# Linear attention and gated convolution on one core: transposes of Q and K in 64-row form into two PSUM banks, steps moved between engines, zero fills as steps, a new order

## The chip, the core and the metric

The kernel runs on one NeuronCore of a Trainium2 chip. The metric is the device time of one execution in microseconds (us), as the median of several runs. The engines are TensorE (PE, with its weight loads as PEld), VectorE (DVE), ScalarE (ACT), GpSimd (POOL) and SyncE (SP). Each works through its own instructions in order and waits for the others by semaphores. Loads that change fp32 to bf16 are issued from POOL's queue; stores are issued from SP's.

## The reference

B = 8 batches, H = 8 heads, S = 576 tokens, D = 64, F = 128 features. The first half is an attention with feature maps, the second a gated unit with a causal convolution of five taps:

```python
def phi(x):
    proj = np.einsum('bhsd,df->bhsf', x, w_phi)
    proj = proj - np.max(np.abs(proj), axis=-1, keepdims=True)
    return np.concatenate([np.exp(proj), np.exp(-proj)], axis=-1)
q_p, k_p = (phi(q), phi(k))
kv = np.einsum('bhsf,bhsd->bhfd', k_p, v)
z = np.sum(k_p, axis=2)
num = np.einsum('bhsf,bhfd->bhsd', q_p, kv)
den = np.einsum('bhsf,bhf->bhs', q_p, z)[..., None] + 1e-06
...
for k in range(K):
    gate_pre += conv_w[k][None, None, :] * xp[:, k:k + S, :]
gate = 1.0 / (1.0 + np.exp(-gate_pre))
val = x @ w_val
return (gate * val @ w_out).astype(np.float32)
```

x is the attention's output, num / den, with the heads side by side (8 x 64 = 512 columns).

## The kernel before

**Units.** Two heads of one batch make a unit (`hp` 0 to 3 in a batch, so 32 units, numbered batch x 4 + `hp`). Of a head's 576 tokens, each of 64 partitions holds 9 neighbouring ones; the two heads of a unit fill the 128 partitions. Eight of the nine token planes go through the unit steps; the ninth planes of a batch's four units go together through steps with an `e` in their names. A number behind a step's name is its unit; for the `e` steps, loads and the second half it is the batch.

**The steps of a unit.** `T` (line 335) transposes its K and Q on PE: eight products of 128 columns against the identity `ident`, into one PSUM bank as bf16. `Tc` copies the 1024 columns to SBUF. `PK` and `PQA` (line 348) multiply by `W2` (w_phi twice, one copy for each half of the rows) with tokens on the partitions. From these DVE takes the largest absolute value of each token: `mKa`, `mKb` for the two banks of K, `mQ` for Q (all line 365). ACT makes `Ka`, `Kb` (line 429), the exponentials of K, each step two instructions, and `E` (line 414), the scales by the maxima. `V` on POOL (lines 454 and 458) multiplies V with the scales. `KV` (line 476) is the product of K's features and V; its last operand, for the ninth planes, is a tile `VZ` of which half must be zero (memsets in line 214). `KVM` copies the result to SBUF. For Q, `PQa` and `PQb` (line 518) make the features with features on the partitions; a nop on SP (`WQ`) stands between them because different row halves write one bank. `DMQ` (line 400) spreads the maxima of Q on a doubled identity `id64`, `SH` (line 534) subtracts them by a product that accumulates, and `Qp`, `Qm` (line 548) are the exponentials. `NUM` (line 566) multiplies Q's features with the copy of `KV`; `RCP` and `XN` on DVE divide; `XP` (line 596) transposes and `XC` copies into `XT`, the input of the second half.

**The second half**, one per batch: `HL` copies the last tokens of the planes in `XT` to where the convolution reads them (SBUF to SBUF). `GA` (line 767) is the convolution as 80 small products, `THx` and `THy` (line 791) the gate on ACT, `VA` (line 802) the product with w_val, `GV` (line 823) gate times value on DVE, `OUT` (line 831) the product with w_out, `OE` (lines 851 on ACT, 853 on DVE) its way out of PSUM, `ST` the store on SP. `WC` brings w_val into another order, SBUF to SBUF.

**What sets the order.** `ORDER` is one text of some 1240 words. Each is a step with its number, behind `@` its PSUM bank or banks, and behind `:` its engine where there is a choice (`P` POOL, `D` DVE, `A` ACT). The program issues the steps in the order of this text, so each engine gets its instructions in that order. `FL` (line 244) is a product that nothing reads, put where PE would be idle. Loads are steps too: `LK`, `LQ`, `LV`, `LE` for a whole batch, `LKa`, `LKb` and so on for parts of the first batch; unit 0's K and Q come first, by other queues (line 195).

Of the kernel before, what the change touches and what calls it, by code (L numbers as in the profile page):

```python
# [29 lines left out]
mQ0 CW0 mKa0 FL13@4 LVa0 Ka0 DMQ0:D Tce1:D mKb0 T1@7 PKe1@4 Kb0 Tc1:D FL15@0 PQA1@6 mQe1 FL6@2 E0 mKe1 KTe1  # L30
mQ1 DG0:P LKb0 PK1@1,2 T4@0 mKb1 PQa0@6 WQ0 PQb0 SH0 Tc4:D FL4@3 T5@0 FL1@3 LE1 DMQ1:D Ka1 PQA4@4 mKa1 Kb1 LE0
V0:P PK4@2,3 Qm0 E1 Qp0 Tc5:D FL19@1 FL12@0 PQA5@6 mKa4 DMQe1:P Ee1 FL18@1 mQ4 PQa1@0 LQb0 PQea1@4 WQ1 PQb1
SH1 Ka4 LV1 FL7@2 Kb4 FL17@2 WQe1 PQeb1 FL11@2 SHe1 DMQ4:D mQ5 Qm1 Qp1 FL8@2 Te0@2 DMQ5:D T2@6 mKb4 Tce0:D Qe1
PKe0@0 PQea0@2 WQe0 Tc2:A mKe0 T3@7 Ee0 mQe0 Ve1:P DMQe0:D E4 V1:P KTe0 PQeb0 FL10@4 FL9@4 PQA2@5 Tc3:D LWV0
SHe0 mQ2 PK2@4,7 FL5@0 Qe0 Ve0:P LVb0 PK3@0,1 KV1@5 mKb2 V4:P PQa4@2 mKb3 WQ4 KV0@6 PQb4 Ka2 Kb2 KVM1:D SH4
mKa2 Kb3 KVM0:D mKa3 PQA3@4 DMQ2:P NUM1@6 mQ3 LWO0 Qm4 RCP1 T6@1 XN1 LK2 KV4@4 PQa2@6 WQ2 E2 PQb2 Qp4 SH2
PQa3@2 E3 DMQ3:D XP1@5 Tc6:D Ka3 WC3:D V2:P NUM0@0 KVM4:D WQ3 PQb3 SH3 XC1:D KV2@4 Qm2 Qp2 V3:P Qp3 PK5@5,6
Qm3 RCP0 WC2:D XN0 KVM2:D XP0@7 KV3@4 mKb5 mKa5 XC0:D NUM2@0 KVM3:A NUM3@2 RCP2 XN2 Ka5 NUMe0@7 PQa5@0 WQ5
# [5 lines left out]
Qm7 Tc9:D mQ8 LK3 RCP6 PKe2@6 E8 XN6 OUT0_2@5 mKe2 NUM7@2 mQe2 LQ3 Tc11:D RCP7 OE0_2:A XN7 OUT0_1@4 KTe2
PQA9@0 PK9@6,7 PQa8@2 WQ8 LQ4 OUT0_0@5 Ee2 OE0_1:A DMQ8:P mQ9 XP7@4 Kb9 mKa9 V8:P XP6@1 OE0_0:A mKb9 T10@0
NUMe1@5 XC6:D Ve2:P XC7:D PQb8 SH8 DMQe2:P RCPe1 XNe1 Ka9 OUT0_3@7 E9 Tc10:D KV8@1 Qp8 PK10@0,6 PQea2@4 WQe2
OE0_3:D Qm8 V9:P KVM8:A XPe1@7 mKa10 PQeb2 SHe2 NUM8@2 XCe1:A DMQ9:P Qe2 KV9@7 PQA10@4 HL1:P mKb10 RCP8 XN8
KVM9:D PQa9@1 LV3 XP8@3 Ka10 mQ10 XC8:D Kb10 WQ9 PQb9 SH9 T12@0 Te3@5 Qp9 GA1@6,3 Tc12:D Tce3:D PK11@0,5 Qm9
# [25 lines left out]
XN20 OUT3_0@5 LV6 Qm21 OUTe1@7 Kb22 mKa22 OEe1:D GA4@0,3 DMQ22:D OE3_0:A Ka22 THx4 PK23@7,6 STe1 Te6@5 mKa23
V21:P THy4 VA4_0@2 E22 mKb23 T24@0 Tce6:D GV4_0 KV21@1 E23 ST2_1 PQa22@4 PQA23@2 Kb23 Tc24:D WQ22 LK7 PQb22
SH22 PK24@6,0 KVM21:D VA4_2@1 Ka23 mQ23 NUM21@2 mKa24 GV4_2 Qm22 RCP21 Kb24 XN21 VA4_3@7 VA4_1@1 LQ7 mKb24
Qp22 V22:P KV22@2 Ka24 XP20@5 XP21@0 V23:P GV4_3 GV4_1 PQa23@6 PQA24@3 KVM22:A LE7 DMQ23:P E24 XC21:A LV7
# [30 lines left out]
def kernel(  # L108
# [102 lines left out]
    for i in range(3):  # L211
        VZs.append(const.tile([P, 2, 2, HP, E1], BF16, name=f"VZ{i}"))
        for h2 in range(2):
            nc.vector.memset(VZs[i][row(h2), :, 1 - h2, :, :], 0.0)
# [761 lines left out]
```

## Time and profile before

| | |
|---|---|
| median of 3 runs | 233.06 us (232.55 to 233.15) |
| profiled execution, own time | 233.09 us |
| its span, first to last instruction | 231.3 us |
| mean granted clock of TensorE | 0.975 |
| instructions of PE / PEld / DVE / ACT / POOL | 3853 / 3888 / 347 / 385 / 192 |
| bytes moved | 26.12 MB |

The span is 1.8 us shorter than the execution's own time. Busy time of PE counts each product until its modelled end, and neighbouring products overlap, so a busy PE isn't yet one at its peak rate. On the other engines, too, an instruction starts a little before the one ahead of it has ended, so a group's busy time is less than its count times its mean. The second part of the page is in 40 slices of 5.8 us each; its row of the granted clock shows full speed but for slices 2 and 3, about 11.6 to 23 us, at half.

### The profile page before, as it was taken

How to read it: one execution, taken by the hardware profiler on the slowest of the kernel's cores; microseconds unless marked ns; L12 is line 12 of the kernel's file. 1: busy time of each engine (PE TensorE's matmuls, PEld its weight loads, DVE VectorE, ACT ScalarE, POOL GpSimd, SP SyncE). 2: the span in 40 equal slices, each digit the busy share in tenths (PEclk: the TensorE clock that was granted, in tenths of full speed). 3: DMA queues.
4: the chain of work that ended last, by engine and by line, in shares of the span. 5: the costliest groups of instructions: out<-in, count | busy, mean ns of one | idle time of the engine just before them, and what ended most of it. 6: DMA issues, size and time to landing. Idle time of an engine off the chain costs nothing.

```text
span 231.3 us, 9094 instructions
## 1 busy us (share of the span) xinstructions
PE 204.6 (88%) x3853; PEld 134.4 (58%) x3888; DVE 198.2 (86%) x347; ACT 192.2 (83%) x385; POOL 158.9 (69%) x192
## 2 busy tenths in 40 slices
...
GB/s 139 213 178 11 138 117 113 114 100 116 38 180 128 167 31 100 127 131 152 172 146 110 105 35 81 18 149 254 206 34 74 94 3 4 27 191 107 95 179 141
DMA packets 27843, 26.12 MB, mean 113 GB/s; under 512 B 5653, under 2 KB 22933, under 8 KB 27802
## 3 DMA queue, kind: packets, MB, share of 16 engines
...
q14 instruction: 11, 0.09, 0.1%
...
## 4 chain that ended last, share of the span: by engine, by line
PE 62%; DVE 17%; ACT 6%; DMA 5%; issue 5%; POOL 1%; DVEq 0%; POOLq 0%; SPq 0%
PE PS L831 11%; PE PS L802 10%; PE PS L348 6%; PE PS L566 6%; DMA kN<-in_k_dram 5%; PE PS L335 5%; PE PS L476 5%; DVE MQ L365 5%; ACT KT L429 3%; PE PS L767 3%; PE PS L518 3%; DVE MK L365 3%; PE PS L596 3%; PE PS L534 2%; DVE XN L586 2%
## 5 line engine op out<-in xcount | busy, mean ns | idle before, releaser
L429 ACT ACTIVATE KT<-PS 128x512 bf16<-128x512 f32 x128 | 68.9, 630 | 10.2 <-DVE MK L365 9.0
L454 POOL TENSOR_TENSOR VT<-vN,E 128x1024 bf16<-128x1024 bf16 x28 | 53.3, 1903 | 26.2 <-ACT E L414 24.1
L548 ACT ACTIVATE QT<-PS 128x1024 bf16<-128x1024 f32 x64 | 64.0, 1064 | 3.1 <-PE PS L683 1.2
L365 DVE TENSOR_REDUCE MK<-PS 128x4 f32<-128x512 f32 x64 | 42.4, 681 | 2.2 <-PE PS L348 1.7
L365 DVE TENSOR_REDUCE MQ<-PS 128x8 bf16<-128x1024 f32 x32 | 39.0, 1218 | 3.8 <-PE PS L348 3.1
L802 PE MATMUL PS<-XT,WVAL 128*128 128x512 bf16 x113 | 30.4, 380 | 1.4 <-issue 0.5
L831 PE MATMUL PS<-WOUT,GV 128*128 128x512 bf16 x113 | 30.3, 380 | 1.0 <-issue 0.3
L400 POOL TENSOR_TENSOR DM<-id,MQ 128x512 bf16<-128x512 bf16 x24 | 25.0, 1042 | 4.6 <-DVE MQ L365 4.3
L348 PE MATMUL PS<-W,T 64*128 64x128 bf16 x512 | 25.0, 220 | 2.8 <-DVE MKe L365 1.0
L476 PE MATMUL PS<-VT,KT 128*128 128x65 bf16 x512 | 24.8, 194 | 2.0 <-DVE KVS L150 1.0
L476 PEld LDWEIGHTS <-KT 128*128 128x128 bf16 x512 | 21.8, 98 | 5.2 <-DVE KVS L150 1.4
L348 PEld LDWEIGHTS <-T 64*128 64x128 bf16 x512 | 16.8, 95 | 12.8 <-issue 8.3
L823 DVE SCALAR_TENSOR_TENSOR GV<-GATE,PS 128x512 bf16<-128x512 bf16 x32 | 21.0, 680 | 3.5 <-ACT GATE L791 3.1
L586 DVE TENSOR_TENSOR XN<-PS,RCP 128x512 bf16<-128x512 f32 x32 | 22.1, 690 | 1.0
L566 PE MATMUL PS<-KVS,QT 128*128 128x65 bf16 x512 | 21.0, 193 | 0.9 <-DVE T L150 0.5
L566 PEld LDWEIGHTS <-QT 128*128 128x128 bf16 x512 | 18.5, 97 | 5.3 <-issue 1.9
L480 PE MATMUL PS<-VZ,KTe 128*128 128x65 bf16 x128 | 21.4, 192 | 0.0
L150 DVE COPY T<-PS 128x1024 bf16<-128x1024 bf16 x30 | 20.4, 682 | 0.4 <-PE PS L335 0.4
L454 POOL TENSOR_TENSOR VZ<-vE,Ee 64x512 bf16<-64x512 bf16 x16 | 16.7, 1042 | 3.1 <-ACT Ee L414 2.4
L518 PE MATMUL PS<-T,W 64*128 64x256 bf16 x128 | 18.0, 278 | 0.6 <-DVE XN L586 0.2
L802 PEld LDWEIGHTS <-WVAL 128*128 128x128 bf16 x128 | 10.9, 97 | 11.7 <-issue 1.2
L791 ACT ACTIVATE GATE<-PS 128x1024 bf16<-128x1024 f32 x16 | 15.7, 1033 | 2.4 <-PE PS L767 2.4
...
## 6 DMA issues: line engine op xcount, KB each, us to landing
...
```

The costliest lines, as they stand in the source:

```text
L348: (nc.tensor.matmul(PS[:, banks[g], jj * F:(jj + 1) * F], T[row(g), n, jj, :, :].rearrange("p a t -> p (a t)"), W2[row(g), :], start=True, ...
L365: nc.vector.tensor_reduce(dst, x, AX.X, ALU.max, apply_absolute_value=True)
L400: engines[eng].tensor_tensor(u.DM[:, :, :], id64[:, :].unsqueeze(1).to_broadcast([P, n, 64]), u.MQ[:, :, :].rearrange("p j g -> p (j g)"). ...
L429: nc.scalar.activation(u.KT[:, ft, par, :, :].rearrange("p b f -> p (b f)"), PS[:, u.PK[par], :], AF.Exp, scale=1.0 if ft == 0 else -1.0,)
L454: engines[eng].tensor_tensor(dst[:, :, :, 0:D], x.unsqueeze(1).to_broadcast([rows, 2, n, D]), e.unsqueeze(3).to_broadcast([rows, 2, n, D]) ...
L476: nc.tensor.matmul(o, u.KT[:, ft, y % 2, h2 * 2 + y // 2, :], u.VT[:, ft, h2 * 4 + y, :], start=(y == 0), stop=False,)
L518: return nc.tensor.matmul(PS[:, u.PQ + a, :].rearrange("p (j g t) -> p g j t", g=2, t=64)[:, g, :, :], W2[row(g), :], u.T[row(g), 1, :, a, :],
L548: nc.scalar.activation(u.QT[:, ft, :, :, :].rearrange("p a n t -> p a (n t)"), half(u.PQ, 512), AF.Exp, scale=1.0 if ft == 0 else -1.0,)
L566: (nc.tensor.matmul(u.NUM[:, jj // 2, x * E1:(x + 1) * E1], u.QT[:, ft, jj // 2, 4 * h2 + 2 * (jj % 2):4 * h2 + 2 * (jj % 2) + 2, :].rearr ...
L586: nc.vector.tensor_tensor(u.XN[:, :, :, :], numview(u)[:, :, :, 0:D], u.RCP[:, :, :].unsqueeze(3).to_broadcast([P, 2, 4, D]), ALU.mult,)
L802: nc.tensor.matmul(PS[:, m.val[r], :], WVAL[:, dt, r, :], xt(b)[:, dt, 4:12, :].rearrange("p n t -> p (n t)"), start=(dt == 0), stop=(dt = ...
L831: nc.tensor.matmul(PS[:, m.out[j], :], m.GV[:, r, j * P:(j + 1) * P], WOUT[:, r, :], start=(r == 0), stop=(r == 3),)
```

## The change

**Transposes.** `T` uses the two halves of the partitions apart: 16 products of 64 columns in place of eight of 128, the products of rows 0 to 63 into one bank and those of rows 64 to 127 into the next. Of each bank 256 words (512 bf16 columns) are used. `Tc` copies the same 1024 columns from two banks.

**Steps moved between engines.** All 32 `DMQ` and the 8 `DMQe` are on POOL (8 and 1 were on DVE), and so is the last `HL` (was on DVE). The four `WC` are on ACT (two were on DVE, two on POOL). `ND`, which makes `id64`, goes from POOL to DVE. Steps that read PSUM move as follows, from DVE to ACT or back: `Tc` on ACT 4 (was 2), `Tce` 3 (0), `KVM` 19 (17), `XC` 4 (8), `OE` 18 (22), `OEe` 3 (2); the rest of each is on DVE.

**Zero fills.** The six memsets of the `VZ` tiles on DVE at the start become three steps `ZV` of two instructions each: two steps on ACT as copies of a zero tile, one on DVE.

**Unread products.** `FL` is called 16 times (was 20), at other places; the eight ahead of the list stay.

**The list** is new as a whole. Its first line before and after, and the diff of the functions:

```diff
-CK0 CQ0 LQ1 T0@5 Tc0:A W0 LKa0 LK1 FL3@2 IF0:D FL2@1 ND0:P PQA0@6 PK0@0,2 FL16@1 FL0@1 FL14@1 LQa0 TP0@1 Te1@3
+LKa0 LK1 FL9@7 LQa0 LQ1 IF0:D LKb0 CK0 LVa0 TP0@4 CW0 DG0:P CQ0 T0@0 ZV0:A Tc0:A ND0:D W0 PQA0@1 mQ0 DMQ0:P
...
         VZs.append(const.tile([P, 2, 2, HP, E1], BF16, name=f"VZ{i}"))
-        for h2 in range(2):
-            nc.vector.memset(VZs[i][row(h2), :, 1 - h2, :, :], 0.0)
...
+    def op_ZV(i, eng):
+        for h2 in range(2):
+            z = VZs[i][row(h2), :, 1 - h2, :, :]
+            if eng == "A":
+                nc.scalar.activation(
+                    z.rearrange("p f h e -> p f (h e)"),
+                    zero[row(h2), 0:HP * E1].unsqueeze(1).to_broadcast([64, 2, HP * E1]), AF.Copy,
+                )
+            else:
+                engines[eng].memset(z, 0.0)
...
     def op_T(i, bank):
         u = units[i]
-        u.Tps = PS[:, bank[0], :].bitcast(BF16)
+        u.Tps = half(bank[0], 256).bitcast(BF16)
+        tv = u.Tps.rearrange("p h (n x a t) -> p h n x a t", n=2, x=2, a=2)
         for n, name in enumerate(("k", "q")):
             for jj in range(4):
-                nc.tensor.transpose(
-                    u.Tps.rearrange("p (n h x a t) -> p n x a h t", n=2, h=2, x=2, a=2)[:, n, jj % 2, jj // 2, :, :],
-                    tok(name, u.b)[:, u.hp, jj * P:(jj + 1) * P], ident[:, :],
-                )
+                for h2 in range(2):
+                    nc.tensor.transpose(
+                        tv[:, h2, n, jj % 2, jj // 2, :],
+                        tok(name, u.b)[row(h2), u.hp, jj * P:(jj + 1) * P], ident[row(h2), row(h2)],
+                    )
...
     def op_Tc(i, eng):
...
-        copy(eng, u.T[:, :, :, :, :].rearrange("p n y a t -> p (n y a t)"), u.Tps)
+        copy(
+            eng, u.T[:, :, :, :, :].rearrange("p n (h x) a t -> p h n (x a t)", h=2),
+            u.Tps.rearrange("p h (n e) -> p h n e", n=2),
+        )
```

POOL at the start of the program, before. `kN` and `qN` are the bf16 tiles of K and Q; 128x576 is one unit's, 128x4x576 a batch's (here batch 1), 128x2x576 the last two units' of batch 0.

```order
L279 DMA qN<-in_q_dram 128x4x576
L279 DMA kN<-in_k_dram 128x576
L279 DMA kN<-in_k_dram 128x4x576
L241 TENSOR_TENSOR id_132<-ident 128x64
L279 DMA qN<-in_q_dram 128x576
L261 TENSOR_TENSOR id_134<-ident 128x32
L262 TENSOR_TENSOR id_134<-id_134,ident 128x32
L263 TENSOR_TENSOR id_134<-id_134,ident 128x32
L264 TENSOR_TENSOR DIAG<-id_134,cwT 128x640
L279 DMA kN<-in_k_dram 128x2x576
L282 DMA vE<-in_v_dram 128x4x64 x2
L454 TENSOR_TENSOR VT<-OS,E 128x16x64
```

The same place after.

```order
L288 DMA kN<-in_k_dram 128x4x576
L288 DMA qN<-in_q_dram 128x576
L288 DMA qN<-in_q_dram 128x4x576
L288 DMA kN<-in_k_dram 128x2x576
L270 TENSOR_TENSOR id_128<-ident 128x32
L271 TENSOR_TENSOR id_128<-id_128,ident 128x32
L272 TENSOR_TENSOR id_128<-id_128,ident 128x32
L273 TENSOR_TENSOR DIAG<-id_128,cwT 128x640
L414 TENSOR_TENSOR DM<-id_126,MQ 128x512 x2
L288 DMA qN<-in_q_dram 128x2x576
L291 DMA vE<-in_v_dram 128x4x64 x2
L414 TENSOR_TENSOR DM<-id_126,MQ 128x512
```

Unit 1's K, issued even ahead of these rows, and its Q now go out before batch 1's Q, which was the first load and is now behind them. The last two units' K of batch 0 go out ahead of `DIAG`, which waits for DVE. Three `DMQ` stand ahead of the first `V`, where there was none.

ACT from its first activation on, before (`qN` and `T` of unit 0, then exponentials `KT`, scales `E`; `KTe` is that of batch 1's ninth planes).

```order
L235 ACTIVATE qN<-QT 128x576
L148 ACTIVATE T<-PS 128x1024
L429 ACTIVATE KT<-PS 128x512 x4
L414 ACTIVATE E<-MK 128x8 x2
L669 ACTIVATE KTe<-PS 128x512 x2
L429 ACTIVATE KT<-PS 128x512 x4
L548 ACTIVATE QT<-PS 128x1024
```

And after.

```order
L244 ACTIVATE qN<-QT 128x576
L233 ACTIVATE VZ_121<-zero 64x2x260 x2
L148 ACTIVATE T<-PS 128x2x2x256
L233 ACTIVATE VZ_123<-zero 64x2x260 x2
L443 ACTIVATE KT<-PS 128x512 x8
L428 ACTIVATE E<-MK 128x8 x4
L443 ACTIVATE KT<-PS 128x512 x4
```

Four zero fills come in, the exponentials of units 0 and 1 stand in one piece, and those of batch 1's ninth planes no longer stand between them.

POOL at the end of the program, before: the last `V` and `DMQ` steps and `HL6` (`XT`).

```order
L454 TENSOR_TENSOR VT<-vN,E 128x16x64
L458 CAST VT<-E 128x16
L150 COPY XT_119<-XT_119 128x4x4x63
L400 TENSOR_TENSOR DM<-id_132,MQ 128x512 x2
L454 TENSOR_TENSOR VT<-vN,E 128x16x64
L458 CAST VT<-E 128x16
L454 TENSOR_TENSOR VT<-vN,E 128x16x64
L458 CAST VT<-E 128x16
```

And after.

```order
L472 CAST VT<-E 128x16
L414 TENSOR_TENSOR DM<-id_126,MQ 128x512
L468 TENSOR_TENSOR VT<-vN,E 128x16x64
L472 CAST VT<-E 128x16
L414 TENSOR_TENSOR DM<-id_126,MQ 128x512
L150 COPY XT_119<-XT_119 128x4x4x63
```

The last `DMQ` now follows the last `V`, and `HL7` is POOL's last instruction; before, it was DVE's.

More of the change, by code (lines that the diff above doesn't have):

```diff
@@ L28 @@
 ORDER = """
-CK0 CQ0 LQ1 T0@5 Tc0:A W0 LKa0 LK1 FL3@2 IF0:D FL2@1 ND0:P PQA0@6 PK0@0,2 FL16@1 FL0@1 FL14@1 LQa0 TP0@1 Te1@3
[L30 to L38, printed above, removed]
@@ L44 @@
[L44 to L48, printed above, removed]
@@ L74 @@
[L74 to L77, printed above, removed]
-PKe6@1 mQ24 XC20:A KTe6 WQ23 PQb23 SH23 Qp23 T25@0 KV23@5 Qm23 Tc25:D NUM22@3 KVM23:D mKe6 ST3_3 OUT4_0@0
@@ L94 @@
-E30 WQ31 GV6_1 V31:P PQb31 SH31 GV6_0 Kb30 V30:P KV31@0 OUT6_2@1 Qp31 Qm31 KVM31:D Qm30 KV30@5 XC29:D KVM30:D
-NUM31@2 Qp30 RCP31 XN31 OUT6_0@0 NUMe7@4 OE6_0:A NUM30@2 RCPe7 XNe7 XP31@5 RCP30 XN30 OUT6_3@6 XPe7@2 XP30@4
-OE6_2:D VAp7_1@7 XC31:A XC30:D XCe7:A VAp7_0@0 HL7:D OE6_3:A OUT6_1@3 GA7@1,4 OE6_1:A VA7_0 THx7 VA7_1 ST5_1
-VAp7_3@6 VAp7_2@3 GV7_0 VA7_3 ST6_1 GV7_1 VA7_2 THy7 GV7_3 OUTp7_2@4 GV7_2 VAe3@5 OUT7_2 OE7_2:A OUTp7_1@3
-OUT7_1 GAe3@0,6 THey3 ST6_3 OUTp7_3@2 OE7_1:D OUT7_3 THex3 OUTp7_0@6 OUT7_0 OE7_3:A GVe3 OUTe3@7 ST7_2 OEe3:A
```

116 lines of the change are left out of this document (70 added, 46 removed).

## The prediction

> **What bounds the kernel now.** First the busy time by stage, from the windows of the trace. The columns are the stretch, its length, the busy time of PE, PEld, DVE, ACT and POOL with the instructions in brackets, the granted clock and DMA's share.
>
> ```profile
> 0.00:17.40 17.40, 7.92 (x56) 3.87 (x58) 8.50 (x19) 4.08 (x5) 8.33 (x18) 0.84 0.98 176
> 17.40:50.00 32.60, 26.68 (x427) 16.88 (x429) 31.26 (x51) 28.53 (x61) 26.25 (x31) 0.93 0.68 105
> 50.00:100.00 50.00, 48.56 (x976) 33.14 (x980) 47.01 (x84) 46.09 (x94) 42.58 (x51) 1.00 0.74 107
> 100.00:150.00 50.00, 47.13 (x954) 32.05 (x963) 47.85 (x84) 47.09 (x95) 38.77 (x46) 1.00 0.62 105
> 150.00:205.00 55.00, 53.98 (x1109) 36.78 (x1118) 51.18 (x89) 52.94 (x110) 39.20 (x45) 1.00 0.51 96
> 205.00:215.00 10.00, 9.89 (x137) 6.05 (x138) 7.76 (x17) 8.46 (x16) 3.80 (x4) 1.00 0.50 135
> 215.00:226.50 11.50, 10.47 (x209) 5.61 (x209) 4.63 (x7) 4.98 (x8) 0.00 (x0) 1.00 0.57 150
> sum 231.30, PE 204.63 PEld 134.39 DVE 198.19 ACT 192.19 POOL 158.92; mean PE 25.58 PEld 16.80 DVE 24.77 ACT 24.02 POOL 19.87
> ```
>
> Three stages. Up to 17.4 us the program waits for data: ACT has worked 4.1 us. From 17.4 to 215 PE, DVE and ACT are all nearly full. DVE is at 96% in the first third (31.26 of 32.6) and at 93 to 96% up to 205; ACT is at 88%, then 92, 94 and 96%. ACT's idle time from 17.4 to 215 is 4.1 + 3.9 + 2.9 + 2.1 + 1.5 = **14.5 us**, and 8.0 of it lie before 100 us, where DVE has 4.3 us free out of 82.6. From 215 on PE works off the last batch alone.
>
> Second the chain of waits, for what ends last, and the start of the timeline for the first stage.
>
> ```profile
> PE 62%; DVE 17%; ACT 6%; DMA 5%; issue 5%; POOL 1%; DVEq 0%; POOLq 0%; SPq 0%
> ...
> 15.68 0.42 PE L621 MATMUL PS<-ident,kN 128*64 128x128 bf16 x4 [6.21 <-DMA kN<-in_k_dram]
> ...
> 17.48 1.09 ACT L429 ACTIVATE KT<-PS 128x512 bf16<-128x512 f32 x2 [6.00 <-DVE MK L365]
> ```
>
> PE has 62% of the chain because its queue is in order and full; it isn't at its peak throughout, so I don't take it for the only bound. At the start the transposes of batch 1's ninth planes stand ahead of unit 1's; PE, and behind it DVE and ACT, wait 6 us for batch 1's K.
>
> **The change, engine by engine.** Durations are means of groups of one shape, from the trace (last columns: count, busy time, mean ns).
>
> ```profile
> L400 DVE TENSOR_TENSOR DM<-id,MQ 128x512 bf16<-128x512 bf16 x8 | 8.4, 1052 | 0.1
> L400 DVE TENSOR_TENSOR DMe<-id,MQe 128x256 bf16<-128x256 bf16 x1 | 1.2, 1232 | 0.0
> L150 DVE COPY WVAL<-GV 128x512 bf16<-128x512 bf16 x2 | 2.2, 1120 | 0.0
> L214 DVE MEMSET VZ<- 64x520 bf16 x6 | 3.0, 492 | 0.8
> L150 DVE COPY T<-PS 128x1024 bf16<-128x1024 bf16 x30 | 20.4, 682 | 0.4 <-PE PS L335 0.4
> L150 DVE COPY Te<-PS 128x512 bf16<-128x512 bf16 x8 | 3.3, 413 | 4.7 <-PE PS L621 4.7
> L150 DVE CAST KVS<-PS 128x260 bf16<-128x260 f32 x15 | 6.2, 414 | 1.6 <-PE PS L480 1.6
> L150 DVE COPY XT<-PS 128x512 bf16<-128x512 bf16 x24 | 9.8, 414 | 0.5 <-PE PS L596 0.5
> L853 DVE TENSOR_SCALAR OS<-PS 128x512 f32<-128x512 f32 x10 | 6.8, 684 | 2.3 <-PE PS L831 2.1
> L429 ACT ACTIVATE KT<-PS 128x512 bf16<-128x512 f32 x128 | 68.9, 630 | 10.2 <-DVE MK L365 9.0
> L148 ACT ACTIVATE T<-PS 128x1024 bf16<-128x1024 bf16 x2 | 2.2, 1098 | 0.5 <-PE PS L335 0.5
> L148 ACT ACTIVATE XT<-PS 128x512 bf16<-128x512 bf16 x8 | 4.8, 616 | 0.7 <-PE PS L596 0.7
> L148 ACT ACTIVATE KVS<-PS 128x260 bf16<-128x260 f32 x17 | 7.1, 435 | 1.9 <-PE PS L480 1.8
> L851 ACT ACTIVATE OS<-PS 128x512 f32<-128x512 f32 x22 | 13.4, 618 | 4.5 <-PE PS L831 4.1 <-POOL VT L458 0.2
> L400 POOL TENSOR_TENSOR DM<-id,MQ 128x512 bf16<-128x512 bf16 x24 | 25.0, 1042 | 4.6 <-DVE MQ L365 4.3
> L400 POOL TENSOR_TENSOR DMe<-id,MQe 128x256 bf16<-128x256 bf16 x7 | 4.3, 613 | 2.4 <-DVE MQe L365 2.2
> L150 POOL COPY XT<-XT 128x1008 bf16<-128x1008 bf16 x7 | 7.2, 1024 | 3.3 <-DVE XT L150 3.3
> L150 POOL COPY WVAL<-GV 128x512 bf16<-128x512 bf16 x2 | 1.2, 622 | 0.0
> L241 POOL TENSOR_TENSOR id<-ident 128x64 bf16<-128x64 bf16 x1 | 0.3, 336 | 0.0
> L150 DVE COPY XT<-XT 128x1008 bf16<-128x1008 bf16 x1 | 0.4, 427 | 0.1
> ```
>
> *DVE* loses 8 DMQ (8.4), 1 DMQe (1.2), 2 WC (2.2), 1 HL (0.4), 4 of 6 memsets (2.0), 2 Tc (1.4), 3 Tce (1.2), 2 KVM (0.8) and 1 OEe (0.7, at OE's 684 ns): 18.3. It gains 4 XC (1.7), 4 OE (2.7) and ND (0.2, guessed below POOL's 336 ns): 4.6. Net **-13.7 us**, to 184.5. By the list, 6 DMQ, the DMQe, both WC and the memsets, 11.8 of the 18.3, lie ahead of batch 1's HL (its row is below). Behind it DVE is hardly lighter: Tc, Tce and KVM leave and XC and OE come.
>
> *ACT* gains four halves of zero fills and four WC. ACT has no SBUF-to-SBUF copy of these shapes; 435 ns (260 columns) and 1098 ns (1024) bound one, and XT's 616 ns at 512 columns is nearest: 4 x 0.62 and 4 x 0.62 = 5.0, with ends of 3.5 and 8.8. Then 2 Tc (2.2), 3 Tce (1.8), 2 KVM (0.9) and 1 OEe (0.6), less 4 OE (2.5) and 4 XC (2.5): net **+5.5 us**, to 197.7. The zero fills lie in the start, where ACT waits anyway.
>
> *POOL* gains 8 DMQ (8.3), a DMQe (0.6) and HL7 (1.0), and loses 2 WC (1.2) and ND (0.3): **+8.4 us**, to 167.3.
>
> *PE.* T was eight products of 128 columns and is now sixteen of 64. Where transposes follow each other, the rows are:
>
> ```profile
> 195.49 0.39 PE L335 MATMUL PS<-ident,kN 128*128 128x128 bf16 x4
> 195.72 0.39 PE L335 MATMUL PS<-ident,qN 128*128 128x128 bf16 x4
> 195.94 0.39 PE L596 MATMUL PS<-ident,XN 128*128 128x128 bf16 x4
> 196.26 0.28 PE L518 MATMUL PS<-T,W 64*128 64x256 bf16 x2
> ...
> 196.59 0.39 PE L348 MATMUL PS<-W,T 64*128 64x128 bf16 x8
> 196.82 0.22 PE L683 MATMUL PS<-Te,W 64*128 64x128 bf16 x2
> ```
>
> Eight products of T take 195.49 to 195.94, 0.45 us. Eight 64-row products of 128 columns (L348) take 0.23 us, from 196.59 to 196.82, so two row halves run side by side. Sixteen of 64 columns thus take 0.23 us if the moving columns set the pace, and 0.46 if the weight loads do (L348's pace for each product). The bounds for 32 units are -7 and 0 us; I take -0.1 each, **-3.2 us** of PE's time, since L348 proves the overlap but not for loads so dense. Four fewer unread products are idle PE time anyway, and count nothing.
>
> The Trainium skill, "TensorEngine Tiling (Array Packing)", Key Properties, says that changing the tiling mode drains TensorE. By that rule the trace agrees: from L596 (128 rows) to L518 (64 rows) are 0.32 us from start to start, against 0.23 between transposes, so 0.09 a change. By the lists, neighbours of different form on PE number 195 before and 199 now: +0.4 us by that rule, 229.6 if all of it reached the end.
>
> *Start.* By the shapes, the first loads in POOL's queue up to batch 1's K, which ended the wait at 15.68, are 576 + 144 + 576 = 1296 KB of bf16; unit 1's Q now stands behind 144 + 576 and ends at 864. In proportion that would be 864/1296 x 15.7, or 10.5 us; since the loads of other queues share the early part, I take about 13 (an estimate; bounds 10.5 and 15.7). Batch 1's first unit (T4) still needs all that stood there before, until about 16. In the gap ACT can do the zero fills (2.5) and Kb0, Ka1 and Kb1 (6 instructions at 68.9/128 = 0.54 of busy time each: 3.2), which it did after 17.4 before. So at 17.4 us ACT has done 4.1 + 2.5 + 3.2 = 9.8 and has 197.7 - 9.8 = 187.9 us left; before it was 192.2 - 4.1 = 188.1. **The early start pays for what ACT takes over and for no more.**
>
> *The middle.* What is left is ACT's idle time. Up to 100 us DVE was full and loses 11.8 us, some 10 of them after 17.4, so its load there falls from 95% to about 83%. ACT's 8.0 us of idle time there can't all go (it also waits for PE and POOL); I take half, -4.0. Behind 100 us DVE and ACT stay as they were, 6.5 us: nothing.
>
> *The end.* HL7 on POOL costs 1.02 in place of 0.43 between the last XC and GA7. A row of the chain gives what products of 512 columns take, 0.22 us each:
>
> ```profile
> 158.39 1.73 PE PS L802 x8
> ```
>
> Behind XP31 the list has OUT6_3 and four products of VA, eight such products or 1.7 us, while XC (0.41) and HL (1.02) take 1.43. That covers them if each of the three handovers takes under 0.1 us; I count +0.3. Without that cover it would be +2.0.
>
> Sum against the profiled execution's own 233.1: -0.2 (ACT's work left) -4.0 + 0.3 = **229.2 us**. The median of the runs is the same to 0.03, so no correction is needed. PE's -3.2 isn't added: it counts only where PE alone is late, and serves as the lower end.
>
> **The rivals.**
>
> *POOL takes DVE's place and the change is slower.* The stretch up to batch 1's HL, and that HL on POOL:
>
> ```profile
> 17.40:74.50 57.10, 50.48 (x888) 33.47 (x892) 55.17 (x93) 52.77 (x111) 48.40 (x59) 0.96 0.71 107
> ...
> 73.49 1.02 POOL L150 COPY XT<-XT 128x1008 bf16<-128x1008 bf16 x1
> ```
>
> POOL gets 6 DMQ and a DMQe more here and loses two WC: +5.6, so 48.4 becomes 54.0 of 57.1. DMQ stands ahead of V in one queue, with loads between, and POOL's old waits of 8.7 us were for ACT's scales and DVE's maxima. It decides once POOL waits more than 3.1 us. With half the old waits HL1 ends 1.3 us later than before, with all of them 5.6: 233.1 + 0.1 (start and end, as above) + 1.3 = 234.5, or 238.8. I price it at 235.5, near the lower end, since unit 1's scales come earlier. For it speaks how full POOL's queue is here; against it that DVE's maxima come sooner once DVE is free.
>
> *The early start carries through.* PE's saving and unit 1's head start both reach the end: 229.2 - 3.2 = 226.0, with ACT at 97% from 17.4 on. For it speaks PE's 62% of the chain; against it that ACT needs all its 187.9 us.
>
> *It only moves idle time.* ACT's idle 14.5 us return at other places, since the orders differ everywhere: 233.1 - 0.2 + 0.3 = 233.2. So would the 64-row form do nothing if weight loads set its pace.
>
> *Two banks hold up PE.* T waits for two free banks in place of one. A wait of 0.1 us a unit would be +3.2 and eat the gain, 232.4; 0.2 gives 235.6. The Trainium skill, "TensorEngine Tiling (Array Packing)", Gotcha 1: PSUM Pressure, states that row tiling raises PSUM pressure because different row tiles write different banks. No run so far has T in that form. Against this rival: T's words stay in PSUM for its 0.45 us and Tc's 0.68, so 32 units take 36 bank-us more, of 8 x 198.
>
> **How the numbers follow.** Forecast (ACT becomes the bound, half its early idle goes) 0.40; early start carried through 0.18; idle time moved 0.14; POOL 0.20; two banks 0.08. A measurement can tell about 0.3%, 0.7 us. Faster: 0.40 + 0.18 + 0.01 = 0.59; same: 0.13; slower: 0.28. The range runs from 224.5 (the early-start case with 1.5 more of PE's bound of 7) to 236.5, which takes in POOL's 235.5 and 1 us above it; the forecast's own range is 227 to 231.5.
>
> **What would show it.** ACT's idle time between 17.4 and 215 near 10 us, DVE at 80 to 85% to 100 us: the forecast. POOL over 95% before HL1, with ACT waiting for PE behind DM: the POOL rival. L346's products: 16 in 0.3 us or 0.46. ACT's copies of WVAL and VZ far from 0.62 us, or unit 1's Q landing after 15 us, would break the start's sum.

## The result and the profile after

| | before | after |
|---|---|---|
| median (range of 4 runs each, on one chip) | 233.09 us (232.55 to 233.15) | 231.1 us (230.74 to 231.24) |
| profiled execution, own time | 233.09 us | 230.74 us |
| its span | 231.3 us | 228.7 us |
| mean granted clock | 0.975 | 0.966 |

The ratio of the two is **0.9917, interval 0.9898 to 0.9936**: 2.0 us faster, where 3.9 were forecast. The two profiled executions differ by 2.35.

The page of the changed kernel, first its busy time and then its chain of waits by engine:

```profile
PE 205.5 (90%) x4140; PEld 128.9 (56%) x4140; DVE 186.4 (82%) x332; ACT 197.2 (86%) x393; POOL 164.5 (72%) x199
...
PE 45%; DVE 24%; ACT 11%; POOL 8%; issue 5%; DMA 2%; SPq 2%; ACTq 0%; DVEq 0%; POOLq 0%
```

The sums of work came out within 2.8 us of the forecast (DVE 186.4 against 184.5, ACT 197.2 against 197.7, POOL 164.5 against 167.3). The chain now passes through more engines, and SP's queue appears in it, which had 0%.

For where the time went, the start of a batch's gate (`THx`) is a mark that both kernels have. The windows of the trace between such marks: 0, 2, 4, 5, 6 and 7, before (the columns are those of the prediction's first view):

```profile
17.40:53.17 35.77, 29.75 (x549) 19.47 (x551) 34.27 (x55) 31.65 (x66) 29.14 (x36) 0.94 0.64 97
53.17:102.67 49.50, 47.95 (x939) 32.00 (x946) 46.43 (x83) 44.91 (x92) 42.35 (x51) 1.00 0.78 115
102.67:152.87 50.20, 47.53 (x959) 32.13 (x968) 48.26 (x85) 48.03 (x98) 38.98 (x45) 1.00 0.65 107
152.87:177.32 24.45, 23.80 (x467) 16.58 (x471) 23.46 (x43) 24.16 (x50) 18.63 (x22) 1.00 0.80 151
177.32:202.34 25.02, 24.65 (x523) 17.13 (x527) 22.22 (x37) 23.25 (x49) 16.18 (x18) 1.00 0.12 29
202.34:216.89 14.55, 14.41 (x251) 8.71 (x253) 10.42 (x22) 11.72 (x23) 5.32 (x6) 1.00 0.47 120
216.89:231.30 14.41, 8.62 (x126) 4.51 (x127) 4.63 (x7) 4.39 (x7) 0.00 (x0) 0.96 0.65 165
```

And after, with the first 17.4 us ahead of them:

```profile
0.00:17.40 17.40, 8.60 (x101) 4.89 (x102) 7.72 (x17) 9.78 (x17) 9.15 (x19) 0.74 0.88 171
17.40:48.92 31.52, 27.34 (x559) 17.29 (x556) 27.52 (x49) 30.76 (x66) 30.26 (x38) 0.93 0.77 112
48.92:98.44 49.52, 47.98 (x1034) 30.70 (x1033) 44.70 (x79) 47.39 (x97) 44.57 (x54) 1.00 0.79 116
98.44:147.27 48.83, 48.33 (x1026) 30.53 (x1023) 45.35 (x79) 46.72 (x95) 37.76 (x44) 1.00 0.71 120
147.27:173.20 25.93, 24.95 (x503) 16.13 (x502) 22.78 (x45) 24.22 (x48) 20.52 (x24) 1.00 0.67 127
173.20:198.48 25.28, 24.50 (x556) 16.15 (x554) 24.01 (x41) 24.25 (x51) 16.78 (x18) 1.00 0.26 42
198.48:214.04 15.56, 15.02 (x258) 8.79 (x255) 9.71 (x20) 9.67 (x19) 5.45 (x7) 1.00 0.44 116
214.04:228.70 14.66, 8.76 (x128) 4.43 (x126) 4.63 (x7) 4.38 (x7) 0.00 (x0) 0.93 0.53 127
```

The first gate starts 4.25 us earlier (48.92 against 53.17), the fifth 5.60 (147.27 against 152.87). Then two stretches are longer than before, by 1.48 (24.45 to 25.93) and 1.01 (14.55 to 15.56), and PE is idle in them for 1.0 and 0.5 us. The end, behind THx7, is longer by 0.25. The gain is made early and partly given back behind 147 us.

What stands in those two stretches, from the timeline of the changed kernel (start, duration, engine, line; in brackets the idle time before and what ended it; SPq is SP's queue):

```profile
168.04 1.33 SPq L945 DMA_DIRECT2D out_dram<-OSe  x2
...
169.48 0.28 PE L532 MATMUL PS<-T,W 64*128 64x256 bf16 x2 [0.91 <-SPq L524]
...
170.02 1.94 ACT L562 ACTIVATE QT<-PS 128x1024 bf16<-128x1024 f32 x2 [0.75 <-PE PS L548]
...
200.34 1.88 SPq L945 DMA_DIRECT2D out_dram<-OSe  x2
...
202.32 0.28 PE L532 MATMUL PS<-T,W 64*128 64x256 bf16 x2 [0.53 <-SPq L524]
...
202.87 1.94 ACT L562 ACTIVATE QT<-PS 128x1024 bf16<-128x1024 f32 x2 [1.23 <-PE PS L548]
```

L524 is the nop on SP (`WQ`) between `PQa` and `PQb`. In the new list two of these nops, `WQ25` and `WQ30`, stand right behind the stores `STe1` and `STe2`. SP is issuing those for 1.3 to 1.9 us, PE waits for the nop, and ACT for PE. Nothing of the kind is in the profile before.

### The profile page after: what moved, and what is told of

The parts are those of the page before. It is cut to its first block, busy times and chain, and to the rows that moved or that the text cites. A ratio compares the mean times of both kernels' runs of the same rounds, so it can differ in the third digit from the quotient of the medians.

```text
span 228.7 us, 9628 instructions
## 1 busy us (share of the span) xinstructions
PE 205.5 (90%) x4140; PEld 128.9 (56%) x4140; DVE 186.4 (82%) x332; ACT 197.2 (86%) x393; POOL 164.5 (72%) x199
## 4 chain that ended last, share of the span: by engine, by line
PE 45%; DVE 24%; ACT 11%; POOL 8%; issue 5%; DMA 2%; SPq 2%; ACTq 0%; DVEq 0%; POOLq 0%
PE PS L845 8%; PE PS L816 7%; DVE MQ L379 5%; PE PS L781 5%; PE PS L362 4%; DVE MK L379 4%; PE PS L490 4%; DVE XN L600 4%; DVE GV L837 4%; ACT KT L443 3%; PE PS L580 3%; DVE T L150 3%; DMA QT<-in_q_dram 2%; POOL VT L468 2%; PE PS L532 2%
## 5 line engine op out<-in xcount | busy, mean ns | idle before, releaser
L443 ACT ACTIVATE KT<-PS 128x512 bf16<-128x512 f32 x128 | 69.7, 638 | 4.3 <-PE PS L362 2.5
L562 ACT ACTIVATE QT<-PS 128x1024 bf16<-128x1024 f32 x64 | 62.9, 1044 | 3.8 <-PE PS L548 3.7
L468 POOL TENSOR_TENSOR VT<-vN,E 128x1024 bf16<-128x1024 bf16 x28 | 53.3, 1903 | 14.6 <-ACT E L428 14.2
L414 POOL TENSOR_TENSOR DM<-id,MQ 128x512 bf16<-128x512 bf16 x32 | 33.3, 1044 | 14.3 <-DVE MQ L379 14.1
L845 PE MATMUL PS<-WOUT,GV 128*128 128x512 bf16 x128 | 32.0, 380 | 0.0
L816 PE MATMUL PS<-XT,WVAL 128*128 128x512 bf16 x128 | 31.2, 380 | 0.2 <-ACT GATE L805 0.2
L362 PE MATMUL PS<-W,T 64*128 64x128 bf16 x512 | 26.1, 226 | 5.8 <-ACT T L148 1.9
L150 DVE COPY T<-PS 128x1024 bf16<-128x1024 bf16 x28 | 19.1, 685 | 2.1 <-PE PS L346 2.0
L580 PEld LDWEIGHTS <-QT 128*128 128x128 bf16 x512 | 17.9, 97 | 5.1 <-issue 1.8
L532 PE MATMUL PS<-T,W 64*128 64x256 bf16 x128 | 18.5, 283 | 2.3 <-SPq L524 1.4
L468 POOL TENSOR_TENSOR VZ<-vE,Ee 64x512 bf16<-64x512 bf16 x16 | 16.7, 1043 | 3.6 <-ACT Ee L428 3.0
L816 PEld LDWEIGHTS <-WVAL 128*128 128x128 bf16 x128 | 11.2, 97 | 12.2 <-issue 1.3
```

The costliest lines, as they stand in the source:

```text
L362: (nc.tensor.matmul(PS[:, banks[g], jj * F:(jj + 1) * F], T[row(g), n, jj, :, :].rearrange("p a t -> p (a t)"), W2[row(g), :], start=True, ...
L414: engines[eng].tensor_tensor(u.DM[:, :, :], id64[:, :].unsqueeze(1).to_broadcast([P, n, 64]), u.MQ[:, :, :].rearrange("p j g -> p (j g)"). ...
L443: nc.scalar.activation(u.KT[:, ft, par, :, :].rearrange("p b f -> p (b f)"), PS[:, u.PK[par], :], AF.Exp, scale=1.0 if ft == 0 else -1.0,)
L468: engines[eng].tensor_tensor(dst[:, :, :, 0:D], x.unsqueeze(1).to_broadcast([rows, 2, n, D]), e.unsqueeze(3).to_broadcast([rows, 2, n, D]) ...
L562: nc.scalar.activation(u.QT[:, ft, :, :, :].rearrange("p a n t -> p a (n t)"), half(u.PQ, 512), AF.Exp, scale=1.0 if ft == 0 else -1.0,)
L580: (nc.tensor.matmul(u.NUM[:, jj // 2, x * E1:(x + 1) * E1], u.QT[:, ft, jj // 2, 4 * h2 + 2 * (jj % 2):4 * h2 + 2 * (jj % 2) + 2, :].rearr ...
```

## The experiments

All are compared with the kernel before on the same chip; e1 to e8 ran on one chip, e9 to e12 on another. Where the text gives a difference from the changed kernel, it is that of the medians, and the ratios give up to 0.7 us more or less. "The stretch to THx5" means from THx4 to THx5. Stretches in the text go from gate to gate; the bounds of the rows shown for e5, e6, e7, e10 and e11 lie up to 0.2 us beside the gates.

| run | median us | ratio to before, interval |
|---|---|---|
| changed kernel | 231.1 | 0.9917, 0.9898 to 0.9936 |
| e1 stores later | 230.57 | 0.9914, 0.9872 to 0.9956 |
| e2 T in 128-row form | 234.8 | 1.0086, 1.0056 to 1.0115 |
| e3 SBUF steps back on DVE | 243.4 | 1.0451, 1.0406 to 1.0496 |
| e4 load order back | 234.27 | 1.0057, 1.0028 to 1.0086 |
| e5 before, 20 more products | 235.29 | 1.0074, 1.0050 to 1.0099 |
| e6 after, 20 more products | 233.71 | 1.0004, 0.9979 to 1.0030 |
| e7 after, 20 more on ACT | 232.75 | 0.9968, 0.9947 to 0.9989 |
| e8 after, 20 more on DVE | 247.77 | 1.0603, 1.0565 to 1.0641 |
| e9 no unread products | 231.54 | 0.9922, 0.9899 to 0.9945 |
| e10 stores moved | 230.15 | 0.9873, 0.9853 to 0.9893 |
| e11 before, SBUF steps moved | 235.39 | 1.0111, 1.0085 to 1.0137 |
| e12 no unread products, stores moved | 229.48 | 0.9849, 0.9829 to 0.9868 |

**e1, the stores behind the nops.**

```diff
-V25:P ST4_3 STe1 T27@2 Tc27:D WQ25 PQb25 DMQ25:P SH25
+V25:P T27@2 Tc27:D WQ25 PQb25 DMQ25:P SH25 ST4_3 STe1
-V30:P STe2 DMQ30:P ... DMQ31:P PQb31 SH31
+V30:P DMQ30:P ... DMQ31:P PQb31 SH31 STe2
```

> The changed kernel with three steps of the list moved: ST4_3 and STe1 behind SH25, STe2 behind PQb31 and SH31. In the changed kernel's trace SP is still issuing STe1 and STe2 when the first halves of Q's features of units 25 and 30 are done, 1.4 and 1.0 us before the nop between the halves can run. Theory (the gain of the first third is given back after 150 us because those nops stand behind stores): 1.4 to 2.4 us less than the changed kernel, near 229. Rival (PE and ACT are full there anyway, and the wait only moves): within 0.5 us of 231.1.

The stretches to THx5 and THx7 became 0.95 and 0.70 us shorter, as the theory has it. But the profiled execution stood still once elsewhere, in the stretch to THx6, in the middle of a run of products:

```profile
180.04 0.27 PE L360 MATMUL PS<-W,T 64*128 64x128 bf16 x3 [1.42 <-issue]
```

No semaphore or queue ends this wait, and why it came is open. In this execution it took back what was won. Whether the other executions of e1 stood still like this isn't known, since only one was profiled; the interval of their ratio is wide (0.9872 to 0.9956) and takes in both the changed kernel and e10.

**e10, the same two stores moved again (STe2 as in e1), with ST4_3 left in its place and the last store on ACT's queue.**

```diff
-V25:P ST4_3 STe1 T27@2 Tc27:D WQ25 PQb25 DMQ25:P SH25
+V25:P ST4_3 T27@2 Tc27:D WQ25 PQb25 DMQ25:P SH25 STe1
...
-            nc.sync.dma_start(ov[:, 8, :], groups[c].OS[row(bb), :])
+            (nc.scalar if c == 3 else nc.sync).dma_start(ov[:, 8, :], groups[c].OS[row(bb), :])
```

> The changed kernel with STe1 behind SH25, STe2 behind SH31, and the last store STe3 issued from ACT's queue. Theory, SP's relays WQ25 and WQ30 stand behind store issues and PE waits for them: the stretches between THx4 and THx5 and between THx6 and THx7 become 0.95 and 0.7 us shorter, and the last store goes out at ACT's last instruction (1.2 us earlier): 228.3 to 229.3 in all. If the relays only take the place of other waits: 230.5 to 231.

The windows of its trace, the stretches to THx5 and to THx7:

```profile
148.58:173.57 24.99, 24.92 (x503) 16.23 (x504) 22.70 (x45) 24.09 (x48) 20.39 (x24) 1.00 0.66 129
...
198.85:213.70 14.85, 14.84 (x259) 8.81 (x256) 9.74 (x20) 9.70 (x18) 5.49 (x7) 1.00 0.48 120
```

24.99 against 25.93 and 14.85 against 15.56: the same 1.65 us as in e1, and PE's idle time there is gone. The end is 0.3 shorter, not 1.2; SP still issues other stores until 224.3 us, but whether these hold the end isn't shown. Of the 1.95 us the medians show 1.0 (0.9873 against 0.9917, and the two intervals don't touch). The rest is within the scatter of the stretch from 17.4 us to THx0, which is 31.5 to 32.9 us long in the profiled executions with this start (31.52 in the changed kernel, 32.89 in e10). A fuller granted clock doesn't make it short: the mean clock was 0.993 in e10, whose stretch is long, and 0.966 in the changed kernel. So the SP waits cost 1.65 us in the profiled stretches, and the medians show 1.0 of it and of the end together.

**e2, T in the old form.** The new list with `T` and `Tc` as before.

```diff
-        u.Tps = half(bank[0], 256).bitcast(BF16)
+        u.Tps = PS[:, bank[0], :].bitcast(BF16)
...
-                for h2 in range(2):
-                    nc.tensor.transpose(tv[:, h2, n, jj % 2, jj // 2, :], ...[row(h2), ...], ident[row(h2), row(h2)])
+                nc.tensor.transpose(..., ident[:, :])
```

> The changed kernel with T in its old form: eight products of 128 rows and 128 columns into the first of the two banks, Tc from one bank; list unchanged. Theory (the new form saves PE 0.15 to 0.2 us a unit, but the order and not PE sets the time over the first two thirds, as the forecast counted): 0 to 2 us more than the changed kernel. Rival (PE is the bound, so the form carries the gain): 4 to 6 us more, slower than the kernel before.

3.7 us slower than the changed kernel, spread over the program (0.4 to 0.7 in each stretch up to THx6, 0.1 in the one to THx7, nothing behind it). Of this 0.7 lies ahead of THx0, where the scatter is as large, 1.2 between THx0 and THx2, and 1.95 between THx2 and THx7. The same place in both, first the changed kernel:

```profile
118.12 0.29 PE L346 MATMUL PS<-ident,kN 64*128 64x64 bf16 x8
118.24 0.30 PE L346 MATMUL PS<-ident,qN 64*128 64x64 bf16 x8
118.35 0.29 PE L532 MATMUL PS<-T,W 64*128 64x256 bf16 x2
```

and e2:

```profile
120.14 0.38 PE L342 MATMUL PS<-ident,kN 128*128 128x128 bf16 x4
120.36 0.39 PE L342 MATMUL PS<-ident,qN 128*128 128x128 bf16 x4
120.68 0.28 PE L525 MATMUL PS<-T,W 64*128 64x256 bf16 x2
```

T takes 0.23 us up to the next step against 0.54. The pace of the columns holds, and in this place a change of form goes too. The rows that the prediction had for such a change (0.09 us) are borne out here: 0.44 us for eight products would be the two halves' 0.22 each, and 0.10 more is spent before L525. Where a step of 128 rows follows, the new form brings a change of form in place of saving one, and gains less: 0.34 us (163.53 to 163.87 in the changed kernel) against 0.45 (167.24 to 167.69 in e2).

**e3, the SBUF-only steps back on DVE.**

```diff
-DMQ0:P DMQ1:P DMQ3:P DMQ4:P DMQ5:P DMQ6:P DMQ16:P DMQ22:P DMQe0:P WC2:A WC3:A WC0:A WC1:A HL7:P
+DMQ0:D DMQ1:D DMQ3:D DMQ4:D DMQ5:D DMQ6:D DMQ16:D DMQ22:D DMQe0:D WC2:D WC3:D WC0:P WC1:P HL7:D
```

> The changed kernel with the SBUF-only steps back where they were: DMQ of units 0, 1, 3, 4, 5, 6, 16, 22 and DMQe of batch 0 on DVE, WC on DVE (two) and POOL (two), HL7 on DVE; list order unchanged. Theory (DVE's relief closes ACT's gaps in the first third, worth some 4 us): 2.5 to 5 us more than the changed kernel, at or above the kernel before. Rival (the earlier start alone brings the gain): within 1 us of 231.1.

12.3 us slower. The `DMQ` instructions on DVE, with minimum, median and maximum, and the window up to THx0:

```profile
L412 DVE TENSOR_TENSOR DM<-id,MQ x8: 683/772/2280, 11.9 to 164.1; 128x512 bf16<-128x512 bf16 x8
```

```profile
17.40:57.32 39.92, 31.06 (x563) 19.16 (x565) 34.95 (x56) 30.18 (x64) 30.89 (x38) 0.92 0.61 89
```

The loss sits where they stand: the stretch up to THx0 grew by 8.4 us, that of `DMQ16` by 3.0, that of `DMQ22` by 0.9, and the others by 0.7 at most. Up to THx0 the moved steps add 7.4 us to DVE's busy time (34.95 against 27.52). About half of that is their own time and half is a wait, an estimate from their shortest durations: five of the eight `DMQ` take 0.68 to 0.85 us, the longest 2.28. What the long ones wait for, e8 shows.

**e8, 20 small copies more on DVE.** One ahead of `RCP` of units 8 to 27, with no data that anyone needs.

```diff
+    def op_DX(i):
+        nc.vector.tensor_copy(spare[:, :], zero[:, 0:224])
```

> The changed kernel with 20 more small copies on DVE (128x224 of zeros into a spare tile, one ahead of RCP of units 8 to 27), at an estimated 0.2 us each, 4 us in all. Both theories: DVE has 13 us of idle time from THx0 to THx7, so under 1 us, 231 to 232. If the time rises by 3 us or more, each of the three engines is on the chain in turn and none is the bound alone.

Neither was right: 16.7 us slower than the changed kernel, though its DVE is idle for 18.6 us from THx0 to THx7 (12.9 in the kernel before). The 20 copies took 19.2 us in place of 4. Their durations with minimum, median and maximum, and from the timeline two of them with what POOL did:

```profile
L241 DVE COPY spare<-zero x20: 205/880/3408, 69.0 to 203.6; 128x224 bf16<-128x224 bf16 x20
```

```profile
176.87 1.90 POOL L471 TENSOR_TENSOR VT<-vN,E 128x1024 bf16<-128x1024 bf16 x1 [0.35 <-ACT E L431]
176.97 1.87 DVE L241 COPY spare<-zero 128x224 bf16<-128x224 bf16 x1
178.71 0.25 POOL L475 CAST VT<-E 128x16 bf16<-128x16 f32 x1
...
181.58 0.21 DVE L241 COPY spare<-zero 128x224 bf16<-128x224 bf16 x1
```

With POOL idle the copy takes 0.21 us. Started 0.1 us behind a 1.90 us instruction of POOL, it takes 1.87 and ends with it. POOL's own instructions are no longer than in the changed kernel (1.90). So a DVE copy between two tiles in SBUF waits for POOL's instruction, and everything behind it on DVE waits too. The Trainium skill, "SBUF — State Buffer", Who interferes with whom, describes this: DVE and GpSimd share a pair of ports under an exclusive lock, which DVE takes in a copy that uses both its ports; the engine that comes second is blocked for the whole of the other's instruction. These rows agree with it. In e3 a wait of the same kind is seen for `DMQ`: the one of 2.24 us, begun at 32.73, lies beside a `V` of POOL from 32.53 to 34.43 and its cast.

**e4, the load order back.**

```diff
-LKa0 LK1 FL9@7 LQa0 LQ1 IF0:D
+LQ1 LKa0 LK1 FL9@7 LQa0 IF0:D
```

> The changed kernel with batch 1's Q (LQ1) again as the first load of POOL's queue, so that unit 1's Q ends behind 1440 KB, not 864. Theory (the early start gives ACT some 3 us of exponentials in the gap, which pay for what it takes over): 2 to 3.5 us more than the changed kernel. Rival (unit 1 waits for a PSUM bank and for DVE until 12 us in any case, and the later units' loads set the pace): within 1 us.

3.2 us slower than the changed kernel, all of it up to THx0 (34.60 us from 17.4 on against 31.52, so 3.1; the later stretches agree to 0.1), as its theory had it. PE's largest wait in its trace:

```profile
PE PS L344 <- DMA qN<-in_q_dram: 4.0, 1, 4.0
```

Unit 1's Q arrives at 14.95 there. In the changed kernel T reads it at 12.30 without a wait for it.

**e5 and e6, 20 more products on PE,** one unread product ahead of `NUM` of units 8 to 27, in the kernel before and in the changed one.

```diff
-NUM8@6
+FL28@6 NUM8@6
...
```

> The kernel before, with 20 more products that nothing reads (128x512, one ahead of NUM of units 8 to 27, into NUM's own first bank, so between the gates of batches 0 and 6). At 0.216 us each (1.73 for eight in the chain of before) they are 4.3 us of PE's time. Theory A, PE is the bound from the first gate on, in the kernel before too (its idle time from THx0 to THx7 is 5 us of 164): most of it reaches the end, 236 to 237.5 us. Theory B, as forecast (PE has room to spare, DVE and ACT set the pace): under 1 us reaches the end, 233 to 234.

> The changed kernel with the same 20 unread products ahead of NUM of units 8 to 27. Theory A, PE is the bound: 231.1 + 3.5 to 4.3 = 234.6 to 235.4. Theory B, ACT is the bound, as forecast (ACT is busy 95% of this stretch): under 1 us, 231 to 232.

The windows from THx0 to THx6 of the kernel before, of e5, of the changed kernel and of e6:

```profile
53.17:202.34 149.17, 143.94 (x2878) 97.83 (x2903) 140.37 (x246) 140.35 (x287) 116.14 (x134) 1.00 0.63 104
```

```profile
52.33:203.85 151.52, 149.00 (x2929) 99.43 (x2927) 140.45 (x246) 140.94 (x287) 116.15 (x134) 1.00 0.62 102
```

```profile
48.92:198.48 149.56, 145.75 (x3107) 93.52 (x3105) 136.84 (x241) 142.58 (x288) 119.63 (x138) 1.00 0.65 107
```

```profile
49.11:200.63 151.52, 149.21 (x3127) 95.18 (x3122) 137.72 (x242) 143.10 (x289) 119.64 (x138) 1.00 0.64 106
```

Of the 4.3 us added, 2.35 reach the end of the stretch before and 1.96 after; without a change there, e4 repeats this stretch to 0.04 us. Neither theory holds whole: PE passes on about half.

**e7, 20 small copies more on ACT,** one ahead of `Qp` of units 8 to 27.

```diff
+    def op_AX(i):
+        nc.scalar.activation(spare[:, 0:32], zero[:, 0:32], AF.Copy)
```

> The changed kernel with 20 more small copies on ACT (128x32 of zeros into a spare tile, one ahead of Qp of units 8 to 27), at an estimated 0.2 us each, 4 us in all. Theory A, PE is the bound: ACT's idle time takes most of it, 231 to 232.3. Theory B, ACT is the bound: 234 to 235.

```profile
50.53:200.77 150.24, 145.93 (x3104) 93.65 (x3101) 137.31 (x242) 144.09 (x309) 119.59 (x138) 1.00 0.66 107
```

The test was weaker than planned: the copies take 0.25 us each, but neighbouring instructions on ACT overlap, and ACT's busy time rose by 1.5 us only, not by 4. The stretch grew by 0.7. That is about half as well. PE and ACT each passed on about half of a small load; neither is the bound alone.

**e9, no unread products in the list.** All 16 `FL` are left out.

> The changed kernel without the 16 unread products FL of its list (the eight ahead of the list stay): 16 x 0.216 = 3.5 us less for PE, most of it before the second gate. As forecast for the four that went (they are idle PE time): 231.1, within 0.5. Theory A, PE is the tightest engine and passes on about half of what it gains or loses: 229.3 to 230. A third way: they keep the granted clock up, and without them it falls: over 231.5, with a lower mean clock than 0.966.

No difference (0.9922 against 0.9917). Where `FL` stands PE had been waiting, as the prediction took it; the granted clock didn't fall with them gone (0.948 to 0.999 in its six executions, 0.965 to 0.998 in the four of the changed kernel).

**e11, the kernel before with only the SBUF steps moved.** Its list and its T are untouched.

```diff
-DMQ0:D DMQ1:D DMQ3:D DMQ4:D DMQ5:D DMQ6:D DMQ16:D DMQ22:D DMQe0:D WC2:D WC3:D WC0:P WC1:P HL7:D
+DMQ0:P DMQ1:P DMQ3:P DMQ4:P DMQ5:P DMQ6:P DMQ16:P DMQ22:P DMQe0:P WC2:A WC3:A WC0:A WC1:A HL7:P
```

> The kernel before, with its own list and its T, and only the SBUF-only steps moved as in the change: eight DMQ and one DMQe from DVE to POOL, four WC to ACT, the last HL to POOL. As forecast (DVE is the bound up to 100 us, its relief takes half of ACT's idle time there): 229 to 230. The rival that POOL takes DVE's place: 234.5 to 239. If DVE had room for them where the old list put them (five of eight DMQ took their short 0.7 us there): 232.5 to 234.

2.2 us slower than before, inside the rival's range. POOL's largest waits here (us in total, times, longest):

```profile
POOL VT L452 <- ACT E L412: 22.8, 16, 4.6
POOL DM L398 <- DVE MQ L363: 15.7, 8, 5.6
```

and in the changed kernel:

```profile
POOL VT L468 <- ACT E L428: 14.2, 9, 2.7
POOL DM L414 <- DVE MQ L379: 14.1, 6, 4.0
```

DVE gains room and can't use it. The window of e11 up to THx0:

```profile
17.40:55.70 38.30, 30.50 (x544) 20.74 (x544) 27.94 (x47) 32.41 (x68) 33.17 (x41) 0.90 0.62 94
```

DVE is idle for 10.4 of 38.30 us there; before it was 1.5 of 35.77. All of the loss is in this stretch. Over the whole program POOL now waits 15.7 us for DVE's maxima, where the kernel before waits 4.3, and the `V` steps stand behind these `DMQ` in its queue. Up to THx0 PE waits for POOL's `V` and `DMQe` steps, 4.4 us in all, which it did not in the kernel before.

**e12, e9 and e10 together.**

> The changed kernel without its 16 unread products and with the stores moved as in the run with STe1, STe2 and STe3 moved. If both work and add up: 226.5 to 228. If the products do nothing: 228.3 to 229.3, the time of the stores alone.

229.48 us, the lowest median of all. Its interval (0.9829 to 0.9868) overlaps with e10's, so that the products' leaving adds anything isn't shown.

## Why the prediction was wrong

The time lies inside the stated range and the direction is right, but half of the forecast gain is missing: 2.0 us in place of 3.9.

**The step that failed** is "Behind 100 us DVE and ACT stay as they were, 6.5 us: nothing". The sum let ACT's idle time fall by 4.0 us up to 100 us and stay as it was behind that. From the rows above, ACT's idle time from 17.4 us to THx2 fell from 8.7 to 2.9 us, by 5.8. But from THx2 to THx7 it rose from 7.1 to 10.7, by 3.7. These late stretches take 115.6 us in the changed kernel and 114.2 before: 1.4 lost where nothing was forecast.

The new wait for SP's queue makes 1.65 us of this. The prediction followed what stands in POOL's queue in the new list; it didn't follow SP's, where stores and nops stand in one row. With the two stores behind the nops (e1, e10) these stretches lose 1.65 us and are 0.3 shorter than before. That this is close to nothing is luck, since T's new form alone saves 1.95 there (e2). Something else in the new order must cost some 1.7 us (115.6 + 1.95 - 1.65 - 114.2); no run shows what. In the last of these stretches, in e10, PE is busy for 14.84 of 14.85 us: there PE is the full engine, and not ACT (9.70 us).

**T's products** were a term put at zero: "it counts only where PE alone is late". e2 gives 3.7 us by the medians, and 3.1 behind THx0 in the profiled executions. The size was too small as well: -0.1 a unit was chosen between 0 and -0.22, and `T` gains 0.31 us where a 64-row step follows and 0.11 where a 128-row step does. The sixteen products themselves take 0.23 us, which is the bound at -0.22. The premise behind the zero, that ACT becomes the bound, is refuted by e5, e6 and e7: PE and ACT each passed on about half of what was added. The profile before had shown it, had one looked at the stretches between gates: PE's idle time from THx0 to THx7 is 163.72 - 158.34 = 5.4 us (sums of the rows above), less than that of DVE or ACT. The trace before also lacks 35 records of products (3853 beside 3888 weight loads), so PE looked somewhat emptier than it was.

**The -4.0 up to 100 us** came true as a number, but partly by luck. THx2 starts at 98.44 in place of 102.67, 4.2 us earlier, for -4.2 with the start's term. The load order gives 3.1 of it (e4) and T's form 1.2 to 1.9 (e2), and together they make all of it. In the sum T's form stood at nothing, and the load order's share was set off against ACT's new work. So, if the parts add up, the new order with the moved steps gives nothing there on balance. Of the signs named beforehand, DVE is at 89% there ((27.52 + 44.70) / 81.04) and not at 80 to 85, and ACT is idle for 13.6 us up to THx7, not for 10. DVE's relief is not enough to close ACT's gaps: with the same steps moved in the old list (e11) ACT is idle for 11.2 us up to THx2, more than the 8.7 before, and the kernel is 2.2 us slower. The new list is not enough either: with the steps back on DVE (e3) ACT is idle for 12.5 us there and the kernel is 12.3 us slower. So these steps have no price of their own. What they cost depends on the order, and the order on where they are.

**The start** was sized well. ACT had done 9.78 us of work at 17.4 (8.6 to 9.7 in five other runs with this start), for 9.8 forecast; unit 1's Q was there by 12.3, for about 13; the zero fills took 0.63 us and `WC` 0.68, for 0.62. ACT had 187.4 us left, for 187.9. e4's 3.1 us, all ahead of THx0, are about the 3.2 us of exponentials that the gap was to take. That ACT's new work takes back as much ("and for no more") isn't shown: no run leaves out that work alone.

**The end** was forecast at +0.3, for the last HL on POOL ahead of GA7. The HL lies beside products of VA, as worked out:

```profile
211.58 1.02 POOL L150 COPY XT<-XT 128x1008 bf16<-128x1008 bf16 x1 [6.83 <-DVE XT L150]
211.68 1.03 PE L816 MATMUL PS<-XT,WVAL 128*128 128x512 bf16 x4
212.64 1.05 PEld L781 LDWEIGHTS <-DIAG 32*32 32x32 bf16 x80 [0.42 <-issue]
```

It cost nothing: from the start of the last XC to GA7 are 1.62 us in both kernels (211.02 to 212.64 here, 213.88 to 215.50 before). The +0.25 that the end did lose lies behind THx7, after this place, so that the two numbers agree by chance.

**The rivals,** with a window and a group of the changed kernel below. POOL's place as the bound did not come: it was at 53.5 of 57.1 us in the stretch up to 74.5, for 54.0 forecast, and even at 30.26 of 31.52 us up to THx0, which got shorter all the same. The new order halved POOL's wait for the scales (29.6 before, 14.2 after), while its wait for DVE's maxima rose from 4.3 to 14.1 us. In the old order the rival's mechanism does come, with PE waiting for POOL, and at about the price it was given (e11), though POOL is not over 95% busy there but at 87% (33.17 of 38.30 us). "It only moves idle time" was half right: of the 5.8 us of ACT's idle time that went, 3.7 came back later. Two banks cost little: the first half of T's products waits for 1.7 us in all 32 units (the last row below; e2, with one bank, 1.1). The unread products were rightly counted as nothing (e9).

```profile
17.40:74.50 57.10, 52.08 (x1053) 33.05 (x1048) 50.39 (x91) 55.31 (x113) 53.50 (x65) 0.96 0.75 103
```

```profile
L346 PE MATMUL PS<-ident,kN 64*128 64x64 bf16 x256 | 10.1, 194 | 1.7 <-DVE MQ L379 1.0 <-ACT QT L562 0.6
```

What stays open: taken by stretches, the parts leave a remainder. Between THx0 and THx2 both kernels take 49.5 us, though T's form saves 1.2 there, and the 1.7 us behind THx2 come on top. So the new order costs about 2.9 us from THx0 to THx7 beside SP's waits, if the parts add up, and no run shows where. e11's +2.2 us can't be counted for it: they arise in the old list, and ahead of THx0.
